# Sums of squares in one bf16 record each, and a scheduler that reckons with longer transfers

## The chip, the cores and the metric

The kernel runs on one core of a Trainium2 chip. The metric is the device time of one execution in microseconds; the median of three runs counts.

## What is computed

Attention with capped scores, then a gated feed-forward block with a token shift, then a block that mixes tokens by a rotated copy of the input. Batch 4, 12 heads, sequence 448, head size 64, model width 768, inner width 1024.

```python
scores = cap * tanh(q @ k.T / sqrt(64) / cap)
x = softmax(scores) @ v                       # heads side by side: (4, 448, 768)
xk = mu_k * x + (1 - mu_k) * x_prev           # x_prev: x one token earlier
xr = mu_r * x + (1 - mu_r) * x_prev
x = sigmoid(xr @ w_r) * (relu(xk @ w_k) ** 2 @ w_v)
theta = x @ w_theta
u = x + w_tok_r @ (x * cos(theta)) + w_tok_i @ (x * sin(theta))
out = u + relu(u @ w_ch)
```

## The kernel before, in words

The weights arrive as 64-bit words that hold floating-point numbers of double width. `group` loads a block of 768 KB (512 KB for w_v), rebases the high halves (`bits`, L455 on ScalarE, L457 on POOL, L459 on VectorE), and forms f32 values with three VectorE operations (L462, L465, L468). It then needs the size of the block: the sum of its squares. Where `early` is set (w_k, and v of the first batch) `grams` forms products of the values with themselves on TensorE in bf16 (L483), VectorE takes the diagonal's sum (L487), and a matmul with a matrix of ones adds over the partitions and gives every partition the total (L489). Elsewhere `squares` has ScalarE square the values with an accumulating column for each part (L496), and one f32 matmul for each column, accumulated, does the same (L501): one part for w_r, w_th and w_ch, two for w_v and for v of the later batches, seven for the token matrices. `size` (L508 to L512) takes a power of two from the exponent of that total; only the magnitude matters. With it the block is split into two f16 parts (L301, L296 or L305 for the first, L545 for the second).

All sums use one PSUM tile (`c_ps`), which the softmax sums (L678, L682, L714) share. Every product with a weight is three f16 matmuls of 448 columns: L785 to L787 for w_k, w_r and w_v, L959 to L961 for w_theta, L989 to L991 for the token matrices, L1011 to L1013 for w_ch. The scores and the products with v are f32 matmuls (L651, L655, L700, L703, L726, L729).

Two word buffers (`w_s`) serve all loads of words in turn. The results of the first phase (squared k, gate z, product x) go to memory and come back later (kd, zd, xd).

The order of everything comes from a planner that runs when the kernel is built. Each operation is registered with `op`: its engine, or a choice of engines, its duration, a rank, and the buffers it reads and writes. `Plan.order` plays the operations through in time, taking for each engine that is free the ready operation of lowest rank; DMA operations go one after the other through a pipe (`moved`), and their consumers are ready `LAT["DMA"]` after the transfer is through. The resulting sequence is issued as it stands: each engine, and SP's queue, which issues nearly all transfers, works through its part in that order. The durations in `op` thus set no time on the chip, but they set the order.

The lines that decide about transfers and about the sums:

```python
LAT = {"PE": 0.2, "ACT": 0.16, "DVE": 0.15, "POOL": 0.16, "DMA": 1.6, "SYS": 0.0}
issue = self.ISSUE.get(got.name, 0.48)
moved = max(t + issue, moved) + got.dur
heapq.heappush(events, (moved + self.LAT[e], seq, 1, got))
```

Of the kernel before, what the change touches and what calls it, by code (L numbers as in the profile page):

```python
# [10 lines left out]
BF16 = mybir.dt.bfloat16  # L11
U32 = mybir.dt.uint32
AF = mybir.ActivationFunctionType
ALU = mybir.AluOpType
# [67 lines left out]
class Plan:  # L82
# [3 lines left out]

    LAT = {"PE": 0.2, "ACT": 0.16, "DVE": 0.15, "POOL": 0.16, "DMA": 1.6, "SYS": 0.0}
    COLS = {"av": 1.0}
# [194 lines left out]
def body(nc, tc, exact, first, qk, v, cap, mu_k, mu_r, w_k, w_v, w_r, w_th, w_tr, w_ti, w_ch, out):  # L283
# [55 lines left out]
    unit = cpool.tile([128, 1], F32, name="unit")  # L339
    nc.gpsimd.memset(unit, 1.0)  # L340
    ones = cpool.tile([128, 3, 2, 32], F32, name="ones")
    nc.gpsimd.memset(ones, 0.0)
# [106 lines left out]
    def bits(rank, h, l, f, into, n, word, fb, res, after=()):  # L449
# [22 lines left out]
        return op("DVE", v1(n), rank, b3, r=[fb, word], w=[res], name="wb3")  # L472

    def grams(rank, parts, d):


        ps = Buf(c_ps)
        for i, sub in enumerate(parts):
            def gram(i=i, sub=sub):
                for k, (_, val, n, w) in enumerate(sub):  # L480
                    x = val().bitcast(BF16).rearrange("p (n two) -> p n two", two=2)[:, :, 1]
                    for c in range(0, n, w):
                        nc.tensor.matmul(ps.t[0:w, 0:w], x[:, c:c + w], x[:, c:c + w], start=(i == 0 and k == 0 and c == 0),  # L483
                                         stop=(i == len(parts) - 1 and k == len(sub) - 1 and c == n - w))
            op("PE", sum(0.06 * (n // w) for _, _, n, w in sub) + 0.1, rank, gram, r=[b for b, *_ in sub], w=[ps], name="gram")
        w = parts[0][0][3]
        op("DVE", v1(128), rank, lambda: nc.vector.scalar_tensor_tensor(out=junk[0:w, 0:w], in0=ps.t[0:w, 0:w], scalar=1.0, in1=ident[0:w, 0:w], op0=ALU.mult, op1=ALU.mult,  # L487
                                                                             accum_out=d.t[0:w]), r=[ps], w=[d], name="tiny")
        op("PE", 0.3, rank, lambda: nc.tensor.matmul(ps.t[:, 0:1], unit[0:w].to_broadcast([w, 128]), d.t[0:w], start=True, stop=True), r=[d], w=[ps], name="bcast")  # L489
        return ps  # L490

    def squares(rank, parts, d, after=()):

        ps = Buf(c_ps)
        for a, (f, val, n, dead, place) in enumerate(parts):
            op("ACT", act(n) + 0.19, rank, lambda a=a, val=val, place=place: nc.scalar.activation(out=place(), in_=val(), func=AF.Square, accum_out=d.t[:, a:a + 1]),  # L496
               r=[f] if f not in dead else [], w=[*dead, (d, a)], after=after, name="norm")

        def total():
            for a in range(len(parts)):  # L500
                nc.tensor.matmul(ps.t[:, 0:1], unit.to_broadcast([128, 128]), d.t[:, a:a + 1], start=(a == 0), stop=(a == len(parts) - 1))  # L501
        op("PE", 0.2 + 0.1 * len(parts), rank, total, r=[d], w=[ps], name="bcast")
        return ps
# [12 lines left out]
    def group(rank, src, dst, m, inv, nb, after=(), early=False):  # L516
# [3 lines left out]
        for a in range(len(dst)):  # L520
            w, f = Buf(w_s), Buf(f_s)
            vals.append(f)

            def half(i, w=w):
                return w.t[:, 0:2 * n].bitcast(U32).rearrange("p (n two) -> p n two", two=2)[:, :, i]

            def val(f=f):
                return f.t[:, 0:n]

            def ld(w=w, a=a):  # L530
                nc.sync.dma_start(out=w.t[:, 0:2 * n].bitcast(U32).rearrange("p (i n) -> p i n", i=nb),
                                  in_=src[n * a:n * a + n, 256 * m:256 * m + 256].rearrange("(i p) n -> p i n", p=128))
            op("DMA", 0.03 + n / 350, rank - 12, ld, w=[w], after=[o_open1], name="wld")
            bits(rank, lambda h=half: h(1), lambda h=half: h(0), val, val, n, w, f, f)
            parts.append((f, val, n, 128) if early else (f, lambda val=val: val().rearrange("p (i t n) -> p i t n", i=nb, t=2), n, [(dst[a], (m, 0)), (dst[a], (m, 1))],
                                                                     lambda a=a: dst[a].t[:, :, :, 128 * m:128 * m + 128].bitcast(F32)))
# [25 lines left out]
    for b in range(B):  # L562
# [4 lines left out]
        for c in range(2):  # L567
            t = Buf(w_s)
            op("DMA", 0.03 + n / 700, R - 10, lambda t=t, c=c, vb=vb: nc.sync.dma_start(out=t.t, in_=vb[:, c * n:(c + 1) * n]), w=[t], after=[o_open1], name="ldm")
            parts.append([(t, lambda t=t: t.t, n, 128)] if b == 0 else (t, lambda t=t: t.t, n, [t], lambda t=t: t.t))  # L570
# [21 lines left out]
    def inputs(g):  # L592
# [4 lines left out]
        else:  # L597
            op("DMA", 1.3, A - 30, lambda: nc.sync.dma_start(out=t.t, in_=qk[g].rearrange("p (t s) -> p t s", t=2)), w=[t], after=[o_open1], name="ldqk")
        vn = vnb[g] = Buf(vn_s)
        op("DMA", 0.8, A - 14, lambda: nc.sync.dma_start(out=vn.t[0], in_=v[g].rearrange("p (h c d) -> p h c d", h=2, c=KC)), w=[(vn, 0)], after=[o_open1], name="ldv")  # L600

# [6 lines left out]
    def largest_scores(g):  # L608
# [21 lines left out]
        def halves():  # L630
            for i in range(2):
                nc.sync.dma_start(out=mb.t[1][64 * i:64 * i + 64], in_=md[g].t[:, SH * i:SH * i + SH].rearrange("h (o s) -> o h s", o=1).to_broadcast([64, 2, SH]))
        op("DMA", 0.65, A + 5, halves, r=[md[g]], w=[(mb, 1)], name="rbi")

# [156 lines left out]
    for b in range(B):  # L791
        def taps(i):
            return [((hi, lo), lambda hi=hi: hi.t, lambda lo=lo: lo.t) for hi, lo in (mixed[i, b, j] for j in range(KD))]
        for m, ps in units("kmm", b, wk, KF, taps(0), PAIR * NP * (b + 1), gone, PAIR * NP / 14):
# [10 lines left out]
            op({"ACT": act(S) + 0.09, "DVE": v1(S)}, 0, 0.0, sq, w=[a, (acc[b], m)], name="sq")  # L805
            kend.append(op("DMA", 0.65, 0.0, lambda a=a, t=kd[b][m]: nc.sync.dma_start(out=t.t, in_=a.t), r=[a], w=[kd[b][m]], name="dst"))
        for m, ps in units("rmm", b, wr, KD, taps(1), PAIR * NP * (b + 1 + KF / 14), gone, PAIR * NP / 14):
            o_ = Buf(tmp_s)
            op({"ACT": act(S), "DVE": 0.62}, 0, 0.0, lambda e, ps=ps, o_=o_: copy(e, o_.t, ps.t[:, 0:S]), r=[ps], w=[o_], name="zev")
            op("DMA", 0.65, 0.0, lambda o_=o_, t=zd[b][m]: nc.sync.dma_start(out=t.t, in_=o_.t), r=[o_], w=[zd[b][m]], name="dst")  # L810
        atop = small()
# [53 lines left out]
    def tokens(rank):  # L865
        fo = []
        for i in range(KT):
            raw, f = Buf(w_s), Buf(xf_s)
            parts = {3: ((w_tr, 384, 64, 0), (w_ti, 0, 64, 64))}.get(i, ((w_tr, 128 * i, 128, 0) if i < 3 else (w_ti, 128 * i - 448, 128, 0),))
            for src, r0, rows, p0 in parts:  # L870
                op("DMA", 0.03 + rows * S * 8 / 360e3, rank - 12, lambda src=src, r0=r0, rows=rows, p0=p0, raw=raw: nc.sync.dma_start(
                    out=raw.t[p0:p0 + rows, 0:2 * S].bitcast(U32), in_=src[r0:r0 + rows]), w=[(raw, p0)], after=[o_open1], name="wld")
# [22 lines left out]
    def values(b):  # L895
        scaled(0.0, iv, ia[b], vsc[b])
        k2 = []
        for m in range(KF):
            a, k = Buf(ka_s), Buf(k2_s)
            k2.append(((k,), lambda k=k: k.t[:, 0], lambda k=k: k.t[:, 1]))  # L900
            rk = K20 + 100 * b + m
            op("DMA", 0.65, rk - 100, lambda a=a, t=kd[b][m]: nc.sync.dma_start(out=a.t, in_=t.t), r=[kd[b][m]], w=[a], after=[o_r2], name="lda")
            op(cs(S), 0, rk, lambda e, a=a, k=k, b=b: copy(e, k.t[:, 0], a.t, sa[b].t), r=[a, sa[b]], w=[(k, 0)], after=[o_r2], name="k2h")
            op("DVE", v1(S) + 0.06, rk, lambda a=a, k=k, b=b: nc.vector.scalar_tensor_tensor(
                out=k.t[:, 1], in0=a.t, scalar=sa[b].t, in1=k.t[:, 0], op0=ALU.mult, op1=ALU.subtract), r=[a, (k, 0), sa[b]], w=[(k, 1)], name="k2l")
        for m, ps in units("vmm", b, wv, KD, k2, VM0 + VM1 * b, []):
            z = Buf(z_s)
            op("DMA", 0.65, T2 - 110, lambda z=z, t=zd[b][m]: nc.sync.dma_start(out=z.t, in_=t.t), r=[zd[b][m]], w=[z], after=[o_l2], name="ldz")
            op("ACT", act(S) + 0.1, 1605.2 + 100 * b, lambda z=z, b=b, m=m: nc.scalar.activation(out=z.t, in_=z.t, func=AF.Sigmoid, scale=rho[b].t[:, m:m + 1]),
# [3 lines left out]
               r=[ps, vsc[b]], w=[z], name="x")  # L913
            op("DMA", 0.65, 0.0, lambda z=z, t=xd[b][m]: nc.sync.dma_start(out=t.t, in_=z.t), r=[z], w=[xd[b][m]], name="stx")
            op("DVE", v1(S), 0.0, lambda z=z, b=b, m=m: nc.vector.tensor_reduce(out=xmx[b].t[:, m:m + 1], in_=z.t, axis=AX.X, op=ALU.max, apply_absolute_value=True),
# [23 lines left out]
    def gates(b, ms, rk):  # L939
        for m in ms:  # L940
            x, h = Buf(xg_s), Buf(xs_s)
            xs[b, m] = h
            op("DMA", 0.65, rk - 10, lambda x=x, m=m: nc.sync.dma_start(out=x.t, in_=xd[b][m].t), r=[xd[b][m]], w=[x], after=[o_r2], name="ldx")
            op(cs(S), 0, rk, lambda e, x=x, h=h: copy(e, h.t[:, 0], x.t, sxi[b].t), r=[x, sxi[b]], w=[(h, 0)], after=[o_l2], name="xh")
# [3 lines left out]
    def angles(b, m):  # L948
        rk = T2 + ST * (6 * b + m)
        ps, x = Buf(q_ps), Buf(xf_s)  # L950
        xf[b, m] = x
        op("DMA", 0.65, rk - 25, lambda: nc.sync.dma_start(out=x.t, in_=xd[b][m].t), r=[xd[b][m]], w=[x], after=[o_r2], name="ldx")
        for kk in range(KD):
# [48 lines left out]
    def channels(b, ms):  # L1002
        for m in ms:
# [12 lines left out]
            op(tt(S), 0, rk, lambda e, t=t, x=x: e.tensor_tensor(out=x.t, in0=t.t, in1=x.t, op=ALU.add), r=[t], w=[x], name="res")  # L1016
            fin.append(op("DMA", 0.65, rk, lambda x=x, m=m: nc.sync.dma_start(out=out[m, :, b * S:(b + 1) * S], in_=x.t), r=[x], name="sto"))

# [76 lines left out]
```

## Time and profile before

| | |
|---|---|
| median of three runs | 803.93 us (803.72 to 804.85) |
| profiled execution | 807.98 us, span 806.2 us |
| mean granted TensorE clock | 0.991 |
| TensorE matmul busy | 777.0 us, 96% of the span, 4924 records |
| TensorE weight load busy | 388.7 us, 48% |
| VectorE, ScalarE, POOL busy | 563.5 us (70%), 430.2 us (53%), 105.0 us (13%) |
| DMA engines busy | 46.9% of 16 engines, 114.76 MB moved |
| v loads (256 KB), xd stores, ka loads (224 KB) | 2.7, 2.3, 3.8 us from issue to landing |
| ScalarE's waits for w_ch loads | 19.0 us in five |

Matmuls are pipelined, so the records' busy times overlap and a busy TensorE need not be at its peak. One f32 matmul leaves two records, one f16 or bf16 matmul one. A granted clock of 1.00 is 2.4 GHz; the lower level is 1.2 GHz.

### The profile page before, as it was taken

The page shows a single profiled execution, that of the slowest core. Times are in us where ns is not written, and L with a number is a line of the kernel's source. Part 1 is how long each engine was busy: PE and PEld are TensorE (multiplying, and loading weights), DVE is VectorE, ACT ScalarE, POOL GpSimd, SP SyncE. Part 2 cuts the span into 40 slices and gives each one's busy share as a digit, 9 for nine tenths or more (in the row PEclk, how much of TensorE's full clock was granted, in tenths as well). Part 3 has the DMA queues.
Part 4 walks back from the last instruction along what each step waited for, and adds up shares of the span by engine and source line. Part 5 has one row for each costly group of instructions (what it writes and reads, how often), then busy time and mean ns, then how long its engine had stood idle before and what let it go on. Part 6 is the DMA issues. An engine that isn't in the chain of part 4 may idle for free.

```text
span 806.2 us, 12778 instructions
## 1 busy us (share of the span) xinstructions
PE 777.0 (96%) x4924; PEld 388.7 (48%) x4924; DVE 563.5 (70%) x1023; ACT 430.2 (53%) x653; POOL 105.0 (13%) x114
## 2 busy tenths in 40 slices
PE   5999999999999999999999998999999999999997
PEld 2445455454444444444545544555555555555553
DVE  2878778888787899778866868777655545545531
ACT  4979868678575785655435443454635333232201
POOL 1224312320012031103000110100301000000000
PEclk9999999999999999999999999999999999999999
DMA  7754646336343333403667866553525433334412
GB/s 262 232 192 128 208 146 226 127 115 196 125 149 126 100 123 126 163 35 111 202 196 257 270 212 226 162 160 82 126 51 133 92 92 86 82 75 100 95 34 72
DMA packets 116829, 114.76 MB, mean 142 GB/s; under 512 B 55820, under 2 KB 108824, under 8 KB 116760
## 3 DMA queue, kind: packets, MB, share of 16 engines
q1 hardware_dynamic: 116592, 113.86, 46.9%
q8 instruction: 40, 0.66, 0.4%
q14 instruction: 29, 0.24, 0.1%
q10 hardware_dynamic: 168, 0.01, 0.0%
HBM read 78.98 MB, written 23.86 MB: 128 GB/s over the span
## 4 chain that ended last, share of the span: by engine, by line
PE 82%; DVE 7%; DMA 7%; ACT 2%; issue 1%; SPq 0%; POOL 0%; DVEq 0%; ACTq 0%; POOLq 0%
PE one L785 10%; PE one L787 9%; PE one L786 9%; PE big L655 6%; PE q L991 4%; PE q L990 4%; PE q L989 4%; PE one L726 4%; PE one L1013 3%; PE one L1012 3%; PE one L1011 3%; PE one L700 3%; PE q L960 2%; PE q L961 2%; PE q L959 2%; DMA w<-in_w_ch 2%
## 5 line engine op out<-in xcount | busy, mean ns | idle before, releaser
L664 ACT ACTIVATE th<-big,tsc 128x896 f32<-128x896 f32 x72 | 70.2, 1004 | 30.1 <-PE big L655 29.8
L668 ACT ACTIVATE th<-th,cap_t 128x896 f32<-128x896 f32 x72 | 73.3, 1038 | 0.0
L785 PE MATMUL one<-k,wv 128*128 128x448 f16 x192 | 68.3, 356 | 1.7 <-DVE z L911 1.4
L785 PE MATMUL one<-sl,wk 128*128 128x448 f16 x192 | 68.1, 355 | 1.6 <-ACT g L796 1.2
L787 PE MATMUL one<-sl,wk 128*128 128x448 f16 x192 | 68.1, 355 | 0.5 <-DVE wk L545 0.5
L787 PE MATMUL one<-k,wv 128*128 128x448 f16 x192 | 68.3, 356 | 0.0
L786 PE MATMUL one<-k,wv 128*128 128x448 f16 x192 | 68.3, 356 | 0.0
L786 PE MATMUL one<-sl,wk 128*128 128x448 f16 x192 | 68.0, 354 | 0.2 <-POOL sl L760 0.2
L989 PE MATMUL q<-wo,zt 128*128 128x448 f16 x168 | 59.2, 352 | 0.0
L991 PE MATMUL q<-wo,zt 128*128 128x448 f16 x168 | 59.2, 352 | 0.0
L990 PE MATMUL q<-wo,zt 128*128 128x448 f16 x168 | 59.2, 352 | 0.0
L1015 ACT ACTIVATE z<-one,scal 128x448 f32<-128x448 f32 x24 | 15.1, 628 | 71.8 <-PE one L1013 71.8
L785 PE MATMUL one<-sl,wr 128*128 128x448 f16 x144 | 51.0, 354 | 0.7 <-ACT wr L496 0.4
L787 PE MATMUL one<-sl,wr 128*128 128x448 f16 x144 | 50.7, 352 | 0.7 <-ACT wr L496 0.7
L786 PE MATMUL one<-sl,wr 128*128 128x448 f16 x144 | 50.7, 352 | 0.0
L655 PE MATMUL big<-qk 64*64 64x448 f32 x432 | 50.0, 564 | 0.0
L975 DVE SCALAR_TENSOR_TENSOR cs<-xf,scal,cs 128x896 f32<-128x896 f32 x24 | 27.6, 1149 | 28.9 <-DMA xf<-xd 23.9
L455 ACT ACTIVATE w<-w 128x768 f32<-128x768 f32 (+2 forms) x26 | 21.9, 840 | 41.1 <-DMA w<-in_w_ch 19.0
L720 DVE RECIPROCAL xt<-one 128x448 f32<-128x448 f32 x12 | 35.5, 2958 | 11.7 <-PE one L714 11.7
L1016 DVE TENSOR_TENSOR xf<-z,xf 128x448 f32<-128x448 f32 x24 | 15.0, 624 | 34.7 <-ACT z L1015 34.7
L993 DVE SCALAR_TENSOR_TENSOR xf<-q,scal,xf 128x448 f32<-128x448 f32 x24 | 16.4, 683 | 32.3 <-PE q L991 32.1
L1012 PE MATMUL one<-w_u,wc 128*128 128x448 f16 x108 | 38.1, 352 | 0.0
(204 smaller groups left out, 1752.0 us busy)
## 6 DMA issues: line engine op xcount, KB each, us to landing
qk<-in_qk SPq DMA_DIRECT2D x18, 448.0 KB, 3.8
kd<-g SPq DMA_DIRECT2D x32, 224.0 KB, 3.7
vn<-in_v SPq DMA_DIRECT2D x24, 256.0 KB, 2.7
w<-in_v SPq DMA_DIRECT2D x8, 768.0 KB, 4.3
w<-in_w_k SPq DMA_DIRECT2D x8, 768.0 KB, 5.2
w<-in_w_v SPq DMA_DIRECT2D x12, 512.0 KB, 4.4
zd<-tmp SPq DMA_DIRECT2D x24, 224.0 KB, 1.9
z<-zd SPq DMA_DIRECT2D x24, 224.0 KB, 2.8
```

What stands on the lines that cost most here:

```text
L655: nc.tensor.matmul(ps.t[o, h, 0:S], t.t[p, 1, 128 * c + 64 * i:128 * c + 64 * i + 64], t.t[p, 0], start=True, stop=True)
L664: op("ACT", act(n * S) + 0.08, A + 1 + 1.8 * c, lambda src=src, th=th: nc.scalar.activation(out=th.t, in_=src(), func=AF.Tanh, scale=tsc), ...
L668: op("ACT", act(n * S) + 0.08, A + 3 + 1.8 * c, lambda th=th: nc.scalar.activation(out=th.t, in_=th.t, func=AF.Exp, scale=cap_t), w=[th], ...
L720: nc.vector.reciprocal(out=rs(), in_=rs() if exact else sp.t[:, 0:S])
L726: nc.tensor.matmul(ps.t[64 * h:64 * h + 64, 0:S], vn.t[0][:, h, c], th[c].t[:, h], start=(c == 0), stop=False, skip_group_check=True)
L785: nc.tensor.matmul(ps.t[:, 0:S], wh, xh(), start=(kk == 0), stop=False)
L786: nc.tensor.matmul(ps.t[:, 0:S], wh, xl(), start=False, stop=False)
L787: nc.tensor.matmul(ps.t[:, 0:S], wl, xh(), start=False, stop=(kk == len(xs) - 1))
L989: nc.tensor.matmul(o, z.t[:, 0, i], wo[i].t[:, 0], start=(i == 0), stop=False)
L990: nc.tensor.matmul(o, z.t[:, 1, i], wo[i].t[:, 0], start=False, stop=False)
L991: nc.tensor.matmul(o, z.t[:, 0, i], wo[i].t[:, 1], start=False, stop=(i == KT - 1))
L1012: nc.tensor.matmul(ps.t[:, 0:S], wh, u.t[:, 1], start=False, stop=False)
```

## The change

The matmul that adds over partitions, at L489 and in `squares`, takes bf16 operands in place of f32: a bf16 matrix of ones, and the upper half of the f32 column, read as bf16 (`upper`). Where `squares` has several columns, VectorE first adds them into one, in place of one accumulating matmul for each. The durations that the planner is told for these matmuls go to 0.11. Separately, the planner's `LAT["DMA"]` goes from 1.6 to 2.0, and the durations of most transfers go up by 12 to 21%; those of the transposes, of the small ones and of the v halves stay.

```diff
-    LAT = {"PE": 0.2, "ACT": 0.16, "DVE": 0.15, "POOL": 0.16, "DMA": 1.6, "SYS": 0.0}
+    LAT = {"PE": 0.2, "ACT": 0.16, "DVE": 0.15, "POOL": 0.16, "DMA": 2.0, "SYS": 0.0}
...
+    unitb = cpool.tile([128, 1], BF16, name="unitb")
+    nc.gpsimd.memset(unitb, 1.0)
...
+    def upper(d):
+        return d.t[:, 0:1].bitcast(BF16)[:, 1:2]
...
-        op("PE", 0.3, rank, lambda: nc.tensor.matmul(ps.t[:, 0:1], unit[0:w].to_broadcast([w, 128]), d.t[0:w], start=True, stop=True), r=[d], w=[ps], name="bcast")
+        op("PE", 0.11, rank, lambda: nc.tensor.matmul(ps.t[:, 0:1], unitb[0:w].to_broadcast([w, 128]), upper(d)[0:w], start=True, stop=True), r=[d], w=[ps], name="bcast")
...
-        def total():
-            for a in range(len(parts)):
-                nc.tensor.matmul(ps.t[:, 0:1], unit.to_broadcast([128, 128]), d.t[:, a:a + 1], start=(a == 0), stop=(a == len(parts) - 1))
-        op("PE", 0.2 + 0.1 * len(parts), rank, total, r=[d], w=[ps], name="bcast")
+        if len(parts) > 1:
+            tiny(rank, lambda: nc.vector.tensor_reduce(out=d.t[:, 0:1], in_=d.t[:, 0:len(parts)], axis=AX.X, op=ALU.add), w=[d])
+        op("PE", 0.11, rank, lambda: nc.tensor.matmul(ps.t[:, 0:1], unitb.to_broadcast([128, 128]), upper(d), start=True, stop=True), r=[d], w=[ps], name="bcast")
...
-            op("DMA", 0.03 + n / 350, rank - 12, ld, w=[w], after=[o_open1], name="wld")
+            op("DMA", 0.03 + n / 290, rank - 12, ld, w=[w], after=[o_open1], name="wld")
```

The other durations of transfers, which the planner alone reads:

| transfer | before | after |
|---|---|---|
| whole v for its size (ldm) | 0.03 + n/700 | 0.03 + n/580 |
| qk (ldqk) | 1.3 | 1.5 |
| v of a group (ldv) | 0.8 | 0.9 |
| token matrices (wld) | rows * S * 8 / 360e3 | rows * S * 8 / 300e3 |
| every 224 KB transfer (dst, lda, ldz, stx, ldx, sto) | 0.65 | 0.78 |

## Rows read from the trace of the kernel before

**Rows 1.** The page's chain that ended last: shares of the span by engine.
```profile
PE 82%; DVE 7%; DMA 7%; ACT 2%; issue 1%; SPq 0%; POOL 0%; DVEq 0%; ACTq 0%; POOLq 0%
```
**Rows 2.** Busy us of each engine by stretch, instructions, granted clock, DMA share, GB/s.
```profile
17.00:161.00 144.00, 136.40 (x1229) 70.72 (x1228) 119.04 (x233) 114.70 (x157) 41.60 (x38) 0.96 0.56 182
161.00:370.00 209.00, 208.62 (x1401) 93.44 (x1402) 173.74 (x265) 139.37 (x212) 28.84 (x26) 1.00 0.38 123
370.00:490.00 120.00, 112.95 (x596) 59.20 (x594) 89.83 (x196) 57.09 (x106) 14.25 (x16) 0.99 0.71 226
490.00:800.00 310.00, 310.00 (x1643) 161.15 (x1642) 176.55 (x313) 111.41 (x172) 18.01 (x13) 1.00 0.40 99
...
480.00:500.00 20.00, 16.92 (x81) 8.33 (x80) 16.67 (x46) 7.38 (x12) 2.77 (x3) 0.91 0.69 233
```
**Rows 3.** TensorE's waits: line, what released it, us in total, times, longest.
```profile
PE one L483 <- DMA w<-in_v: 4.4, 1, 4.4
...
PE q L960 <- DVE xs L945: 3.0, 1, 3.0
PE one L678 <- DVE scal L508: 1.8, 3, 1.3
PE one L501 <- ACT wr L496: 1.6, 1, 1.6
...
PE one L489 <- DVE junk L487: 1.2, 3, 0.4
```
**Rows 4.** The chain that ended last, in order of time, 370 to 495 us.
```profile
469.32 8.20 DMA w<-in_w_ch
```
**Rows 5.** ScalarE's timeline, 455 to 486 us: start, duration, instruction, [idle before].
```profile
477.55 0.91 ACT L455 ACTIVATE w<-w 128x768 f32<-128x768 f32 x1 [4.68 <-DMA w<-in_w_ch]
```
**Rows 6.** Groups of instructions by line: the sums' records.
```profile
L501 PE MATMUL one<-scal,unit 128*128 128x1 f32 x86 | 11.9, 232 | 2.2 <-ACT wr L496 1.6 <-DVE scal L508 0.3 <-ACT wc L496 0.3
...
L489 PE MATMUL one<-scal,unit 128*128 128x1 f32 x18 | 3.2, 249 | 1.2 <-DVE junk L487 1.2
```
**Rows 7.** TensorE's timeline: a gram, and four sums with what follows each.
```profile
28.24 0.52 PE L483 MATMUL one<-f 128*128 128x128 bf16 x6
...
96.59 0.38 PE L489 MATMUL one<-scal,unit 128*128 128x1 f32 x2
96.90 0.98 PE L655 MATMUL big<-first 64*64 64x448 f32 x8
...
117.97 0.28 PE L489 MATMUL one<-scal,unit 128*128 128x1 f32 x2
118.11 0.35 PE L785 MATMUL one<-sl,wk 128*128 128x448 f16 x1
...
135.89 0.50 PE L501 MATMUL one<-scal,unit 128*128 128x1 f32 x4
136.25 0.35 PE L785 MATMUL one<-sl,wr 128*128 128x448 f16 x1
...
430.40 1.62 PE L501 MATMUL one<-scal,unit 128*128 128x1 f32 x14
432.09 0.35 PE L785 MATMUL one<-k,wv 128*128 128x448 f16 x1
```
**Rows 8.** Groups of instructions by line: VectorE's reciprocal and smallest reduction.
```profile
L720 DVE RECIPROCAL xt<-one 128x448 f32<-128x448 f32 x12 | 35.5, 2958 | 11.7 <-PE one L714 11.7
...
L423 DVE TENSOR_REDUCE scal<-scal 128x1 f32<-128x8 f32 (+2 forms) x9 | 1.4, 157 | 0.4 <-ACT g L802 0.3
```
**Rows 9.** DMA issues: KB each, median us from issue to landing.
```profile
qk<-in_qk SPq DMA_DIRECT2D x18, 448.0 KB, 3.8
...
w<-in_w_k SPq DMA_DIRECT2D x8, 768.0 KB, 5.2
...
w<-in_w_th SPq DMA_DIRECT2D x6, 768.0 KB, 4.4
w<-in_w_ch SPq DMA_DIRECT2D x6, 768.0 KB, 7.6
```

More of the change, by code (lines that the diff above doesn't have):

```diff
@@ L568, in body @@
             t = Buf(w_s)
-            op("DMA", 0.03 + n / 700, R - 10, lambda t=t, c=c, vb=vb: nc.sync.dma_start(out=t.t, in_=vb[:, c * n:(c + 1) * n]), w=[t], after=[o_open1], name="ldm")
+            op("DMA", 0.03 + n / 580, R - 10, lambda t=t, c=c, vb=vb: nc.sync.dma_start(out=t.t, in_=vb[:, c * n:(c + 1) * n]), w=[t], after=[o_open1], name="ldm")
             parts.append([(t, lambda t=t: t.t, n, 128)] if b == 0 else (t, lambda t=t: t.t, n, [t], lambda t=t: t.t))
@@ L597, in inputs @@
         else:
-            op("DMA", 1.3, A - 30, lambda: nc.sync.dma_start(out=t.t, in_=qk[g].rearrange("p (t s) -> p t s", t=2)), w=[t], after=[o_open1], name="ldqk")
+            op("DMA", 1.5, A - 30, lambda: nc.sync.dma_start(out=t.t, in_=qk[g].rearrange("p (t s) -> p t s", t=2)), w=[t], after=[o_open1], name="ldqk")
         vn = vnb[g] = Buf(vn_s)
-        op("DMA", 0.8, A - 14, lambda: nc.sync.dma_start(out=vn.t[0], in_=v[g].rearrange("p (h c d) -> p h c d", h=2, c=KC)), w=[(vn, 0)], after=[o_open1], name="ldv")
+        op("DMA", 0.9, A - 14, lambda: nc.sync.dma_start(out=vn.t[0], in_=v[g].rearrange("p (h c d) -> p h c d", h=2, c=KC)), w=[(vn, 0)], after=[o_open1], name="ldv")
         def halves():
@@ L632, in halves @@
                 nc.sync.dma_start(out=mb.t[1][64 * i:64 * i + 64], in_=md[g].t[:, SH * i:SH * i + SH].rearrange("h (o s) -> o h s", o=1).to_broadcast([64, 2, SH]))
-        op("DMA", 0.65, A + 5, halves, r=[md[g]], w=[(mb, 1)], name="rbi")
+        op("DMA", 0.78, A + 5, halves, r=[md[g]], w=[(mb, 1)], name="rbi")
     def scores(g):
@@ L805, in body @@
             op({"ACT": act(S) + 0.09, "DVE": v1(S)}, 0, 0.0, sq, w=[a, (acc[b], m)], name="sq")
-            kend.append(op("DMA", 0.65, 0.0, lambda a=a, t=kd[b][m]: nc.sync.dma_start(out=t.t, in_=a.t), r=[a], w=[kd[b][m]], name="dst"))
+            kend.append(op("DMA", 0.78, 0.0, lambda a=a, t=kd[b][m]: nc.sync.dma_start(out=t.t, in_=a.t), r=[a], w=[kd[b][m]], name="dst"))
         for m, ps in units("rmm", b, wr, KD, taps(1), PAIR * NP * (b + 1 + KF / 14), gone, PAIR * NP / 14):
@@ L809, in body @@
             op({"ACT": act(S), "DVE": 0.62}, 0, 0.0, lambda e, ps=ps, o_=o_: copy(e, o_.t, ps.t[:, 0:S]), r=[ps], w=[o_], name="zev")
-            op("DMA", 0.65, 0.0, lambda o_=o_, t=zd[b][m]: nc.sync.dma_start(out=t.t, in_=o_.t), r=[o_], w=[zd[b][m]], name="dst")
+            op("DMA", 0.78, 0.0, lambda o_=o_, t=zd[b][m]: nc.sync.dma_start(out=t.t, in_=o_.t), r=[o_], w=[zd[b][m]], name="dst")
         atop = small()
@@ L870, in tokens @@
             for src, r0, rows, p0 in parts:
-                op("DMA", 0.03 + rows * S * 8 / 360e3, rank - 12, lambda src=src, r0=r0, rows=rows, p0=p0, raw=raw: nc.sync.dma_start(
+                op("DMA", 0.03 + rows * S * 8 / 300e3, rank - 12, lambda src=src, r0=r0, rows=rows, p0=p0, raw=raw: nc.sync.dma_start(
                     out=raw.t[p0:p0 + rows, 0:2 * S].bitcast(U32), in_=src[r0:r0 + rows]), w=[(raw, p0)], after=[o_open1], name="wld")
@@ L901, in values @@
             rk = K20 + 100 * b + m
-            op("DMA", 0.65, rk - 100, lambda a=a, t=kd[b][m]: nc.sync.dma_start(out=a.t, in_=t.t), r=[kd[b][m]], w=[a], after=[o_r2], name="lda")
+            op("DMA", 0.78, rk - 100, lambda a=a, t=kd[b][m]: nc.sync.dma_start(out=a.t, in_=t.t), r=[kd[b][m]], w=[a], after=[o_r2], name="lda")
             op(cs(S), 0, rk, lambda e, a=a, k=k, b=b: copy(e, k.t[:, 0], a.t, sa[b].t), r=[a, sa[b]], w=[(k, 0)], after=[o_r2], name="k2h")
@@ L907, in values @@
             z = Buf(z_s)
-            op("DMA", 0.65, T2 - 110, lambda z=z, t=zd[b][m]: nc.sync.dma_start(out=z.t, in_=t.t), r=[zd[b][m]], w=[z], after=[o_l2], name="ldz")
+            op("DMA", 0.78, T2 - 110, lambda z=z, t=zd[b][m]: nc.sync.dma_start(out=z.t, in_=t.t), r=[zd[b][m]], w=[z], after=[o_l2], name="ldz")
             op("ACT", act(S) + 0.1, 1605.2 + 100 * b, lambda z=z, b=b, m=m: nc.scalar.activation(out=z.t, in_=z.t, func=AF.Sigmoid, scale=rho[b].t[:, m:m + 1]),
@@ L913, in values @@
                r=[ps, vsc[b]], w=[z], name="x")
-            op("DMA", 0.65, 0.0, lambda z=z, t=xd[b][m]: nc.sync.dma_start(out=t.t, in_=z.t), r=[z], w=[xd[b][m]], name="stx")
+            op("DMA", 0.78, 0.0, lambda z=z, t=xd[b][m]: nc.sync.dma_start(out=t.t, in_=z.t), r=[z], w=[xd[b][m]], name="stx")
             op("DVE", v1(S), 0.0, lambda z=z, b=b, m=m: nc.vector.tensor_reduce(out=xmx[b].t[:, m:m + 1], in_=z.t, axis=AX.X, op=ALU.max, apply_absolute_value=True),
@@ L942, in gates @@
             xs[b, m] = h
-            op("DMA", 0.65, rk - 10, lambda x=x, m=m: nc.sync.dma_start(out=x.t, in_=xd[b][m].t), r=[xd[b][m]], w=[x], after=[o_r2], name="ldx")
+            op("DMA", 0.78, rk - 10, lambda x=x, m=m: nc.sync.dma_start(out=x.t, in_=xd[b][m].t), r=[xd[b][m]], w=[x], after=[o_r2], name="ldx")
             op(cs(S), 0, rk, lambda e, x=x, h=h: copy(e, h.t[:, 0], x.t, sxi[b].t), r=[x, sxi[b]], w=[(h, 0)], after=[o_l2], name="xh")
@@ L951, in angles @@
         xf[b, m] = x
-        op("DMA", 0.65, rk - 25, lambda: nc.sync.dma_start(out=x.t, in_=xd[b][m].t), r=[xd[b][m]], w=[x], after=[o_r2], name="ldx")
+        op("DMA", 0.78, rk - 25, lambda: nc.sync.dma_start(out=x.t, in_=xd[b][m].t), r=[xd[b][m]], w=[x], after=[o_r2], name="ldx")
         for kk in range(KD):
@@ L1016, in channels @@
             op(tt(S), 0, rk, lambda e, t=t, x=x: e.tensor_tensor(out=x.t, in0=t.t, in1=x.t, op=ALU.add), r=[t], w=[x], name="res")
-            fin.append(op("DMA", 0.65, rk, lambda x=x, m=m: nc.sync.dma_start(out=out[m, :, b * S:(b + 1) * S], in_=x.t), r=[x], name="sto"))
+            fin.append(op("DMA", 0.78, rk, lambda x=x, m=m: nc.sync.dma_start(out=out[m, :, b * S:(b + 1) * S], in_=x.t), r=[x], name="sto"))
     for b in range(B):
```

## Prediction, written before the changed kernel was run

> **What bounds the kernel now.** The chain of waits comes first: TensorE carries 82% of it, transfers 7% and VectorE 7% [rows 1]. So a microsecond counts when it is TensorE's, and only where TensorE isn't waiting for something else. The busy time by stretch says where that is [rows 2]. From 161 to 370 us and from 490 to 800 us TensorE has next to no idle time (209.00 - 208.62 = 0.4 us, and nothing). From 17 to 161 us it idles 144.00 - 136.40 = 7.6 us, beside a VectorE busy for 83% and a ScalarE for 80%; from 370 to 490 us it idles 7.05 us, beside DMA engines busy for 71%. The list of TensorE's waits names the releasers [rows 3]: 4.4 us at the start, which the change doesn't touch, then 3.0 us for xs near 486 us, 1.8 us for the size arithmetic (L508), 1.6 us for a norm of w_r (L496), and a tail of small ones.
>
> **The two large waits.** Both follow a load of words. In the first, ScalarE's rebase of w_r (L455) waits for its load, the square (L496) comes behind it, and TensorE's sum starts 1.6 us late [rows 3]. In the second, a w_ch load is issued at 469.32 us and lands some 8.20 us later [rows 4]; ScalarE, an in-order queue, waits 4.68 us for it until 477.55 [rows 5], with the k copies queued behind, VectorE's halves of k behind those, and then the xs that TensorE needs, 3.0 us late [rows 3]. The slice from 480 to 500 us has a granted clock of 0.91 [rows 2]: part of it ran at the 1.2 GHz level after that idle time, which gives away 20 x 0.09 = 1.8 us more. Together 1.6 + 3.0 + 1.8 = 6.4 us.
>
> **Part 1: the sums' records.** 52 f32 matmuls of one column (18 records at L489, 86 at L501, two to a matmul [rows 6]) become 37 bf16 ones of one record: 9 behind grams, 28 behind squares. The records' own 11.9 + 3.2 us overlap, so I take distances from a sum's start to the next start [rows 7]: a two-record sum costs 0.14 us between f16 matmuls (117.97 to 118.11) and 0.31 us beside f32 ones (96.59 to 96.90); there are 27 of them, by the neighbours about 6.5 us. Nine four-record sums cost 0.36 to 0.53 us (135.89 to 136.25 is typical), 3.6 us. The fourteen-record one costs 1.69 us (430.40 to 432.09). Sum: 11.8 us, of it 4.6 from 17 to 161 us (17 sums), 2.8 from 161 to 370 (7), 4.1 from 370 to 490 (11), 0.3 later (2).
>
> No one-column bf16 sum is in the trace. The nearest row is a gram: six bf16 records of 128 columns take 0.52 us, 0.087 each [rows 7]. Half of the f32 prices is 0.07 and 0.155. I take 0.10 us: 37 x 0.10 = 3.7 us, so 8.1 us less TensorE time (2.9, 2.1, 3.0 and 0.1 by stage). At 0.07 it is 9.2 us; with one record as dear as today's two (37 x 0.25 us) it is 2.6 us.
>
> What of this reaches the end? From 161 to 370 us and after 490 us TensorE never rests: all 2.2 us. In the other two stages it rests 5 to 6% of the time, each time for an engine or a load that a shorter sum doesn't hasten; a sum ahead of such a wait only lengthens the wait. I count half, 5.9 / 2 = 2.95 us; the ends are 0 and 5.9. Part 1 brings **-5.15 us**.
>
> **Part 2: the added reduction.** Ten of the 28 sums behind squares have several columns and get a VectorE reduction first. The nearest one takes 157 ns (L423) [rows 8]: 1.6 us in all, which costs nothing by itself where VectorE has slack (83% busy from 161 to 370 us, where seven of the ten stand). But the sum now waits for VectorE's queue instead of ScalarE alone. Queued ahead there can be an L720 reciprocal of 2958 ns [rows 8], and behind the waiting sum stand all of TensorE's matmuls. The nearest row is the gram's sum, which also waits for a VectorE operation (L487): 1.2 us of TensorE idle over nine sums [rows 3]. So 10 x 0.13 = **+1.3 us**; the ends are 0 and ten waits like the longest of TensorE's for the size arithmetic, 1.3 us each, 13 us [rows 3].
>
> The shared PSUM tile of the sums is freed earlier by the same shortening; the softmax sums that waited 1.8 us for L508 want that tile [rows 3]. I cost it at nothing, since VectorE, whose turn they wait for, gains nothing. At most 1.8 us could go.
>
> **Part 3: the scheduler's transfers.** No instruction is added; the order on every queue is worked out anew: TensorE's, VectorE's, ScalarE's and SP's, and with the choice of engine POOL's too. A 768 KB load is reckoned at 0.48 + 0.03 + 768/290 + 2.0 = 5.16 us instead of 4.30; measured medians are 5.2 (w_k), 4.4 (w_th) and 7.6 us (w_ch). A qk load goes from 3.38 to 3.98 us, measured 3.8 [rows 9]; a v load from 2.88 to 3.38, measured 2.7 (the table of the profile). So the new figures are nearer for the loads of words and of qk, and too long for v. That is what the two large waits ask for: with a later landing reckoned, work that is ready is put ahead of the rebase in ScalarE's queue. But w_ch still lands 2.4 us later than reckoned. I count half of the 6.4 us, **-3.2 us**. The bounds: all of it goes (-6.4), or a new order opens a hole as dear as both in another place (+6.4).
>
> The Trainium skill, "DMA: Bandwidth & Descriptors", section "Latency and other measured facts", gives an HBM access latency of 0.2 us on average and 2 us at high load, and calls it the dominant component of a transfer's fixed cost. The trace agrees in kind: the same 768 KB take 4.4 us as w_th and 7.6 us as w_ch [rows 9]. By that rule one longer constant doesn't follow the crowded stretch, and part 3 would bring nothing; that case is the first rival.
>
> **Sum.** -5.15 + 1.3 - 3.2 = -7.05 us. Durations are from an execution of 807.98 us (span 806.2 us and 1.8 us around it), 4.05 us above the median of 803.93; that execution would come to 800.9, and taken from the median the forecast is 796.9, say **797.0 us**. The terms miss by about 3 us each way in part 1 (none or all of the contested 5.9 us), 3.2 in part 3 (none or all of the 6.4) and 1.5 in part 2; as independent misses that is 4.6 us, so its own range is 792.5 to 801.5.
>
> **Rivals.** First, the loads still land later than reckoned where the DMA engines are crowded; both large waits stay, and only the sums pay: 803.93 - 5.15 + 1.3 = 800.1. For it: 7.6 us for w_ch against 5.16 reckoned. Against: w_r's load, on which the other wait hangs, is like w_k's 5.2 us.
>
> Second, slower: words pass through two buffers, so a load can start only when the conversion two before it has read its words. If conversions are ordered later by the added 0.86 us, each also starts the next load but one later. The 14 loads of w_k and w_r fall before 161 us, where TensorE already waits for what they yield [rows 3]: 14 x 0.86 / 2 = 6.0 us, part 3's gain is gone, and 803.93 - 3.85 + 6.0 = 806.1. It decides the sign once a load is set back by more than 3.85 / 7 = 0.55 us. For it: a w_k load takes 5.2 us [rows 9], and the buffers leave only one other load to overlap it. Against: ScalarE and VectorE have 17 to 20% of slack there [rows 2].
>
> Third, no difference: the savings from 17 to 161 and 370 to 490 us fall into waits wholly and the reductions cost what I took: -2.2 + 1.3 = -0.9, 803.0.
>
> Fourth, everything pays: -8.1 + 1.3 - 6.4 = -13.2, 790.7.
>
> **Chances.** Forecast 0.46, loads still late 0.18, slower conversions 0.17, no difference 0.10, everything 0.09. Of the second rival's neighbourhood some orders are worse than 806.1, so I let the range run from 790.5 to 807. A measurement of this kernel tells 0.2%, 1.6 us, from no change. Faster: 0.46 + 0.09 and 0.15 of the first rival's 0.18, 0.70; within it the third rival and the rest of the first, 0.13; slower 0.17.
>
> **What would show it.** Right, part 1: 37 bf16 records of one column and no f32 one at these lines, under 0.16 us from start to next start, and some 8 us less TensorE busy time. Part 2: TensorE waits on VectorE ahead of the sums of 1 to 2 us in total. Part 3: no TensorE wait of 3 us ahead of the xs matmuls, granted clock 1.00 near 490 us, and ScalarE's waits for w_ch under today's 19.0 us (the table of the profile). Wrong, if TensorE's idle time from 17 to 161 us grows past 7.6 us (slower conversions), if a new wait of several microseconds stands where the w_v or token words are wanted, or if sums stand idle behind reciprocals.

## The result, and the profile after

The changed kernel takes 794.21 us (791.74 to 794.83, four runs) against 804.39 us for the kernel before (803.72 to 805.09): a ratio of 0.9865, 95% interval 0.984 to 0.9891. On a second chip it is 0.9876 (0.9827 to 0.9925, 795.44 against 803.99 us). The forecast was 797.0 us, 7 us less; 8.6 to 10.2 us were measured.

The profiled execution took 794.37 us, its span is 792.5 us. The chain that ended last has moved further to TensorE, at the cost of transfers and VectorE [rows 1]:

```profile
PE 86%; DVE 5%; DMA 4%; ACT 2%; issue 1%; SPq 0%; POOL 0%; ACTq 0%; DVEq 0%
```

Busy time by stretch, with the columns of [rows 2] (the last two are granted clock and DMA, as there):

```profile
17.00:161.00 144.00, 134.10 (x1267) 67.21 (x1260) 118.65 (x230) 120.79 (x167) 44.70 (x39) 1.00 0.57 183
161.00:370.00 209.00, 206.20 (x1344) 88.83 (x1344) 170.00 (x262) 138.07 (x215) 36.72 (x38) 1.00 0.39 127
370.00:490.00 120.00, 117.36 (x614) 60.25 (x613) 95.04 (x221) 60.84 (x111) 9.24 (x11) 0.99 0.73 234
490.00:786.00 296.00, 296.00 (x1569) 153.48 (x1568) 165.19 (x274) 107.21 (x168) 21.45 (x13) 1.00 0.39 97
480.00:500.00 20.00, 20.00 (x111) 10.55 (x109) 16.56 (x47) 7.21 (x13) 1.56 (x2) 1.00 0.53 166
```

TensorE's idle time from 370 to 490 us fell from 7.05 to 2.6 us, and the slice from 480 to 500 us is full, at a clock of 1.00. Against that, idle time from 17 to 161 us grew from 7.6 to 9.9 us, and from 161 to 370 us from 0.4 to 2.8. The list of waits shows which went and which came [rows 3]; here L699 is the spread of the softmax denominators (L694 before), L965 the xs product, L507 the sum behind squares:

```profile
PE one L699 <- DVE rs L694: 5.4, 4, 1.9
PE big L660 <- DMA first<-in_qk: 4.0, 1, 4.0
PE one L489 <- DMA w<-in_v: 2.8, 2, 1.5
PE big L660 <- ACT th L669: 1.4, 1, 1.4
...
PE q L965 <- DVE xs L950: 1.0, 2, 0.5
...
PE one L507 <- DVE scal L513: 0.7, 1, 0.7
```

Both large waits that the prediction named are gone as such (3.0 us for xs is 1.0, the sum's 1.6 us for w_r's square is no longer there). A new one, 5.4 us for the reciprocal of the denominators, has taken the place of waits that came to 0.6 us before.

The sums themselves, by line and then in TensorE's timeline, each with what follows it [rows 6, 7]:

```profile
L507 PE MATMUL one<-scal,unitb 128*128 128x1 bf16 x28 | 4.7, 169 | 0.7 <-DVE scal L513 0.7
...
L506 DVE TENSOR_REDUCE scal<-scal 128x1 f32<-128x2 f32 (+1 forms) x10 | 1.4, 144 | 2.4 <-ACT wo L502 1.7 <-ACT w L502 0.7
...
L495 PE MATMUL one<-scal,unitb 128*128 128x1 bf16 x9 | 1.6, 175 | 0.0
```

```profile
95.42 0.18 PE L495 MATMUL one<-scal,unitb 128*128 128x1 bf16 x1
95.53 0.98 PE L660 MATMUL big<-first 64*64 64x448 f32 x8
...
119.84 0.17 PE L507 MATMUL one<-scal,unitb 128*128 128x1 bf16 x1
119.87 0.35 PE L790 MATMUL one<-sl,wk 128*128 128x448 f16 x1
...
230.40 0.17 PE L507 MATMUL one<-scal,unitb 128*128 128x1 bf16 x1
230.50 0.97 PE L731 MATMUL one<-th,vn 128*64 128x448 f32 x4
```

37 records where there were 104. Between f16 matmuls a sum now costs 0.03 us, beside f32 ones 0.10 to 0.11.

**A sum over the whole span.** Three parts make up a span: TensorE's work at full clock (its busy time less what the lower clock added to it), that clock loss, and idle time. The loss is counted only where TensorE was busy; in both traces the granted clock is low again after the last matmul, and that costs nothing. Kernels with the same sums give 767.9 to 770.2 us of work (52 two-record matmuls, three kernels) and 759.9 to 762.0 (37 one-record ones, eight executions of six kernels): a figure from one execution holds to some 2 us, and a difference of two to some 3.

| | span | busy | clock | work at full clock | clock loss + idle |
|---|---|---|---|---|---|
| before | 806.2 | 777.0 | 0.991 | 770.2 | 6.8 + 29.2 = 36.0 |
| changed | 792.5 | 763.5 | 0.994 | 760.1 | 3.4 + 29.0 = 32.4 |

By these two executions 10.1 us less work and 3.6 us less waiting; by the means of those three and eight, 769.4 and 760.7, it is 8.7 us less work. The steps from each sum's records to the next start, waits left out, come to 10.9 us before and 2.0 in the changed kernel, 8.9 us less. Either way it looks like a gain made by the sums alone. The experiments show that it isn't.

### The profile page after: what moved, and what is told of

It is laid out like the page before. It is cut to its first block, busy times and chain, and to the rows that moved or that the text cites. A ratio compares the mean times of both kernels' runs of the same rounds, so it can differ in the third digit from the quotient of the medians.

```text
span 792.5 us, 12657 instructions
## 1 busy us (share of the span) xinstructions
PE 763.5 (96%) x4857; PEld 374.4 (47%) x4857; DVE 555.2 (70%) x1010; ACT 435.9 (55%) x669; POOL 114.5 (14%) x122
## 4 chain that ended last, share of the span: by engine, by line
PE 86%; DVE 5%; DMA 4%; ACT 2%; issue 1%; SPq 0%; POOL 0%; ACTq 0%; DVEq 0%
PE one L790 12%; PE one L792 11%; PE one L791 11%; PE big L660 6%; PE q L995 4%; PE q L996 4%; PE q L994 4%; PE one L1018 3%; PE one L1017 3%; PE one L1016 3%; PE one L731 3%; PE one L705 2%; PE q L964 2%; PE q L965 2%; PE q L966 2%; DMA w<-in_v 2%
## 5 line engine op out<-in xcount | busy, mean ns | idle before, releaser
L984 POOL TENSOR_TENSOR zb<-cs,zb 128x896 f16<-128x896 f32 x9 | 17.3, 1923 | 169.4 <-DVE zb L303 88.2
L765 POOL TENSOR_TENSOR sl<-mx,sl 128x448 f16<-128x448 f32 x27 | 31.9, 1183 | 67.5 <-ACT sl L299 64.8
```

Of the source, the lines that this page charges most:

```text
L765: op(tt(S, True), 0, R + i, lambda e, t=t, hi=hi, lo=lo: e.tensor_tensor(out=lo.t, in0=t.t, in1=hi.t, op=ALU.subtract), r=[t, hi], w=[lo], ...
```

## The experiments

Two theories stood against each other at first: the sums' work pays (records), or the order worked out with longer transfers pays (order). A third came with them: that any new order lies a few microseconds off the last, and the changed kernel is one draw (luck). All ratios are to the kernel before, run on the same chip.

**Sums alone.** The diff without the lines on transfers.

> The kernel before with the one-record sums alone, planner told their new durations, transfers reckoned as before. Records theory (the sums' TensorE time is what pays, the order is a side effect of either sign): 795 to 799 us. Order theory (the longer transfers make the better order and carry most of the gain): 800 to 804 us. Luck theory (any new order moves the time by several us either way): no value, 794 to 806.

Measured: 800.48 us, 0.9965 (0.9948 to 0.9982). That is inside the range of the order theory, 1.5 us above that of the records theory, and by the ratios 7 to 8 us short of the changed kernel.

**Transfers alone.** The kernel before with

```diff
-    LAT = {... "DMA": 1.6, ...}
+    LAT = {... "DMA": 2.0, ...}
-            op("DMA", 0.03 + n / 350, rank - 12, ld, w=[w], after=[o_open1], name="wld")
+            op("DMA", 0.03 + n / 290, rank - 12, ld, w=[w], after=[o_open1], name="wld")
```

and the other lengths of the table.

> The kernel before with the longer transfers in the planner alone, f32 sums. Records theory: 802 to 806 us, no change that counts. Order theory: 796 to 800 us, and no wait of 3 us for xs near 486 us. My term for this part was -3.2 us: 800.7 us by it.

Measured: 806.21 us, 1.0032 (1.0007 to 1.0058), a little slower. That is outside the range of the order theory. ScalarE's waits for words (L455) did fall, as the change intends: 13.8 us in all, where the kernel before has 39.0. The time didn't follow. In this trace 5.7 us of TensorE idle time stand from 360 to 380 us, where the kernel before has 0.7.

So apart the halves come to 0.9965 x 1.0032 = 0.9997, together to 0.9865.

**One-record sums in the old order.** The planner is told nothing new, so every instruction keeps its place.

```diff
-                nc.tensor.matmul(ps.t[:, 0:1], unit.to_broadcast([128, 128]), d.t[:, a:a + 1], ...)
+                nc.tensor.matmul(ps.t[:, 0:1], unitb.to_broadcast([128, 128]), upper(d, a), ...)
```

> Every instruction in the order of the kernel before; each of the 52 f32 one-column matmuls becomes a bf16 one of one record (two for two parts, seven for seven, so no VectorE reduction is added). By the changed kernel's trace such a sum costs 0.03 us between f16 matmuls and 0.11 beside f32 ones, which leaves about 2.5 of 11.8 us. Records theory with all of it reaching the end: 795 us. With my half of it in the stretches where TensorE waits: 798 to 799 us. Luck theory: 799 or more, since the order is unchanged.

Measured: 800.61 us, 0.9974 (0.9952 to 0.9996). Work at full clock is 762.5 us in this execution, 7.7 us less than in that of before; the time fell by 2.1 us (0.3 to 3.9). By these figures about three quarters of the saved work must have turned into waiting. That is inferred: the two traced executions themselves lie 10.6 us apart, since before's, 807.98 us, is slower than the four runs of the result above (803.72 to 805.09) and this one, 797.39 us, is the second fastest of ten. What they show is that TensorE's idle time from 360 to 500 us is 8.8 us here, where it was 7.05, and that the xs wait of [rows 3] still stands there:

```profile
PE q L965 <- DVE xs L950: 2.8, 1, 2.8
```

**Two-record sums in the new order.** The changed kernel, order and reductions as they are, with f32 operands:

```diff
-    ... nc.tensor.matmul(ps.t[:, 0:1], unitb.to_broadcast([128, 128]), upper(d), start=True, stop=True) ...
+    ... nc.tensor.matmul(ps.t[:, 0:1], unit.to_broadcast([128, 128]), d.t[:, 0:1], start=True, stop=True) ...
```

> Every instruction in the order of the changed kernel, the added VectorE reductions too, but the 37 sums are f32 matmuls of two records. They cost 0.14 to 0.31 us instead of 0.03 to 0.11, 37 x 0.15 = 5.5 us more TensorE time. Records theory: 797 to 800 us. Order theory: 795 to 796 us, hardly above the changed kernel.

Measured: 796.05 us, 0.9916 (0.9891 to 0.9941), between the two ranges. The work is 766.8 us, 6.7 more than with bf16 by these two executions (5.4 by the steps from the sums' records to the next start), yet against the changed kernel's 0.9865 and 0.9876 only 0.4 to 0.5% are lost, 3 to 4 us, with intervals that touch or overlap. The new order with f32 sums and fewer records (37 x 2 for 52 x 2) brings 6.8 us. Those steps come to 7.4 us here and 10.9 in the kernel before, so up to 3.5 of the 6.8 us can be the fewer records' and not the order's.

**Neighbours of the changed kernel.** On one chip: the changed kernel again (0.9876, above), then with only the landing of 2.0, only the longer lengths, and with

```diff
-        op("PE", 0.11, rank, lambda: nc.tensor.matmul(ps.t[:, 0:1], unitb...
+        op("PE", 0.13, rank, lambda: nc.tensor.matmul(ps.t[:, 0:1], unitb...
```

> The changed kernel as it is, beside its neighbours on one chip. All theories: 10 us under the kernel before, ratio 0.984 to 0.989.

> One-record sums, and of the planner's longer transfers only the landing (1.6 to 2.0); the lengths stay as before. Transfers theory (a reckoning nearer to the measured landings shortens the waits for words, whichever half of it): 795 to 798 us, between the sums alone (0.9965 of the kernel before) and the changed kernel. Luck theory (any re-sorted order lies somewhere within some 8 us): no value, 794 to 804.

> One-record sums, and of the planner's longer transfers only the lengths (a sixth more); the landing stays at 1.6. Transfers theory: 795 to 799 us and ScalarE's and VectorE's waits for words between those of the sums alone (31.5 + 11.3 us) and of the changed kernel (19 + 3 us). Luck theory: no value, 794 to 804.

> The changed kernel with the planner told 0.13 instead of 0.11 for each one-record sum, which means nothing on the chip but sorts the work anew in each queue. Transfers theory: within 2 us of the changed kernel, since sums and transfers are as there. Luck theory: 3 to 8 us above it, since the changed kernel is one good draw among many.

Measured: landing alone 799.13 us, 0.992 (0.989 to 0.995); lengths alone 790.21 us, 0.9809 (0.9758 to 0.9859), the fastest of all; 0.13 instead of 0.11 800.86 us, 0.9962 (0.9941 to 0.9984). The transfers theory missed all three: the landing alone came out 1 us above its range, with 42.7 us of ScalarE's waits for words where the sums alone have 31.5, and the lengths alone 5 us below it, below the luck theory's range too. The last one shows what an order without meaning can do: a figure that only the planner reads, changed by 0.02, takes the ratio on that chip from 0.9876 to 0.9962, 5.4 us by the medians and 6.9 by the ratios, most of the changed kernel's gain. Sums and transfers are reckoned as before it; even the waits for words are as low (19.6 us on ScalarE, 18.8 in the changed kernel). What differs is a hole. Busy time from 360 to 400 us with the columns of [rows 2], first the changed kernel, then this one:

```profile
360.00:400.00 40.00, 37.77 (x195) 18.74 (x192) 33.06 (x67) 22.61 (x47) 5.66 (x6) 0.96 0.52 167
...
360.00:400.00 40.00, 30.95 (x158) 15.29 (x156) 32.20 (x67) 24.33 (x51) 6.16 (x6) 0.91 0.46 150
```

TensorE idles 2.2 us there in the one and 9.05 in the other; from 17 to 161 us it is 9.9 and 11.2. TensorE's waits in the kernel with 0.13 from 355 to 420 us:

```profile
PE one L790 <- ACT sl L299: 7.6, 1, 7.6
PE one L791 <- DVE sl L765: 0.5, 1, 0.5
PE one L790 <- DVE tmp L303: 0.4, 1, 0.4
PE one L791 <- POOL sl L765: 0.4, 1, 0.4
```

It stands where attention ends and the second weight product begins: the last token-shift mixes, which the w_k products want, queue on ScalarE and VectorE behind the split of k for the product after it (L301, L909).

**The hole closed by hand.** In that kernel, after planning, the k splits go behind the last mixes in both queues. The edit also moves those loads of k (`lda`) that stood behind the first of these splits, so the expectation's "nothing else moves" doesn't hold for SP's queue.

```diff
+    mix = [o for o in P.ops if o.name in ("mxd", "mxk", "mxh", "mxl")][-7:]
+    lo, hi = seq.index(last1[-1]), max(seq.index(o) for o in mix)
+    k2 = [i for i in range(lo, hi) if seq[i].name in ("k2h", "k2l")]
+    late = [seq[i] for i in range(lo, hi) if i in k2 or (seq[i].name == "lda" and i > k2[0])] if k2 else []
+    seq = seq[:lo] + [o for o in seq[lo:hi + 1] if o not in late] + late + seq[hi + 1:]
```

> The kernel whose planner was told 0.13 for the sums (800.9 us, a hole of 7.6 us in TensorE near 366 us), with one edit of the order after planning: the two f16 parts of k of the next phase that stood ahead of the last token-shift mixes in ScalarE's and VectorE's queues go behind them; nothing else moves. If the order near the border of the phases is what makes that draw bad, the hole falls to 3 to 4 us and the time to 796 to 798 us. If the hole is only where some other lateness shows, it moves and the time stays within 1.6 us of 800.9.

Measured: 804.65 us, 1.0018 (0.9996 to 1.0039), worse instead of better: 3.8 us by the medians, 4.5 by the ratios (the two ran on different chips). TensorE's waits in the same stretch:

```profile
PE one L790 <- ACT g L801: 6.6, 1, 6.6
PE one L790 <- ACT sl L299: 3.7, 1, 3.7
PE one L790 <- DVE tmp L303: 0.4, 1, 0.4
PE one L791 <- POOL sl L765: 0.4, 1, 0.4
```

The hole shrank to 3.7 us as expected, and a larger one opened behind it, where the products' evictions (L801, ScalarE) now stand behind the k splits. My expectation was wrong in its sum: moving work out of the way in one place of an in-order queue put it in the way in the next. ScalarE's queue wasn't full there, though: it idled 3.3 us, as two pairs of splits ahead of that eviction waited for their loads:

```profile
375.55 1.25 ACT L301 ACTIVATE k<-first,scal 128x448 f16<-128x448 f32 x2 [2.31 <-DMA first<-kd]
377.75 1.23 ACT L301 ACTIVATE k<-ka,scal 128x448 f16<-128x448 f32 x2 [0.95 <-DMA ka<-kd]
378.88 0.62 ACT L801 ACTIVATE g<-one,scal 128x448 f32<-128x448 f32 x1
```

The four k loads behind the first four are issued from 373.01 us on, where they were issued from 365.94 on before the edit: k has four buffers, so a load must wait for the splits (L301 and L909) that read its buffer, and it now went back with them. The two holes also cost clock. From 360 to 400 us TensorE idles 11.3 us, and part of the rest runs at the 1.2 GHz level, with f16 matmuls 0.37 us apart instead of 0.19; the granted clock is 0.79 where it was 0.91:

```profile
360.00:400.00 40.00, 28.72 (x132) 13.36 (x131) 29.56 (x56) 21.48 (x44) 5.66 (x5) 0.79 0.41 132
```

Over the whole span idle time even fell, from 34.6 to 33.4 us, and the clock loss of busy time rose from 1.7 to 5.9: by these two executions what the edit cost is the clock's. The runs point the same way: their granted clocks are 0.983 to 0.990, where those before the edit are 0.987 to 0.994.

**The same for the kernel before, and records in the fastest order.** The kernel before with 0.32 and 0.22 + 0.1 for each part in place of 0.3 and 0.2 + 0.1; the lengths-only kernel with f32 sums in its own order; and that kernel again beside them.

> The kernel before, its planner told 0.02 more for each of these sums, which means nothing on the chip. Luck theory: off the kernel before by 2 to 7 us either way, more likely slower, since that one was kept among others. Against it: within 1.6 us.

> The order of the kernel with longer lengths alone (landing 1.6), instruction by instruction, but with f32 sums of two records. Records theory: the 37 second records and their price cost 6.5 us of TensorE time by the accounting of the earlier traces (765.2 against 758.7 us at full clock); in that order TensorE waits least, so most of it reaches the end: 4 to 6 us above its twin with one-record sums. If the order alone made that kernel fast, it is within 2 us of its twin.

> The kernel with one-record sums and longer lengths alone, again, beside its f32 twin. All theories: 0.976 to 0.986 of the kernel before, the fastest of those tried.

Measured: the kernel before re-sorted 808.21 us, 1.005 (1.0026 to 1.0074). Lengths alone 790.01 us, 0.9813 (0.9781 to 0.9844); the same order with f32 sums 790.07 us, 0.9813 (0.9781 to 0.9845). Here the second records cost nothing that can be measured. Busy time of the two from 17 to 161 and from 360 to 500 us, first with f32 sums:

```profile
17.00:161.00 144.00, 137.34 (x1293) 71.76 (x1293) 123.48 (x233) 121.05 (x173) 41.32 (x36) 1.00 0.60 187
...
360.00:500.00 140.00, 134.83 (x717) 71.09 (x715) 110.00 (x251) 66.26 (x119) 19.93 (x22) 0.99 0.68 217
```

then with one-record sums:

```profile
17.00:161.00 144.00, 136.18 (x1279) 68.65 (x1279) 122.58 (x231) 120.73 (x172) 41.07 (x36) 0.99 0.60 187
...
360.00:500.00 140.00, 134.85 (x709) 69.04 (x708) 110.75 (x254) 67.08 (x119) 19.42 (x22) 0.99 0.69 221
```

TensorE idles 6.7 us from 17 to 161 us with f32 sums and 7.8 us with bf16, and 5.2 us from 360 to 500 us with either. Over the whole span the traces give 765.1 us of work with f32, and 760.2 and 762.0 in the two executions of the kernel with bf16: 3.1 to 4.9 us of saved work (the 765.2 and 758.7 of the expectation take off the lower clock where TensorE idled too). The steps from the sums' records to the next start, 7.2 us with f32 and 1.8 with bf16, say 5.3. The spans are 789.8 us against 788.3 and 788.1, so in these executions 1.5 to 1.7 us of it came through, and clock loss and idle time took the rest. The medians, which don't rest on that division, say that all of it came back as waiting, though their intervals leave room for some 3 us either way.

## Why the prediction came out right, point by point

**The direction and the range** held, and the forecast lies 1.6 to 2.8 us off. None of its three terms is borne out at its size: the first brought less in every fixed order, the second cost nothing that shows, and the third brought between what I took and twice that. These misses offset each other, so much of that closeness is chance.

**The sums' work** fell by more than I took: a one-record sum costs 0.03 us between f16 matmuls and 0.10 to 0.11 ahead of f32 ones, not 0.10 throughout, and the work at full clock fell by about 8.7 us (means over executions; 10.1 in the one pair) instead of 8.1. From start to start the 37 sums, their waits left out, come to 2.0 us. The 11.8 us that the prediction has for the sums before is 0.9 too much: by the same steps the 27 two-record sums come to 5.7 us and not 6.5, and 0.2 us of the fourteen-record sum's 1.69 is a wait of the next matmul; all 104 records come to 10.9. **What of it reaches the end** was over-sized at 5.15 us: in a fixed order it is 2.1 us of 7.7 (old order), 3 to 4 of 5.4 to 6.7 (new order, on different chips) and none of 3 to 5 (the fastest order), the times by ratios and medians and the work by single executions. The step that was off is the share: "all of it" where TensorE never rests, and half elsewhere. In the old order the runs can't tell which of the two failed; in the fastest order both did, within the intervals. My reading is that a stretch without idle time is only full because work is there to do; when it is done earlier, TensorE comes earlier to the next thing that it must wait for. The traces bear that out in part: in the old order idle time from 360 to 500 us grew by 1.8 us, in the fastest order that from 17 to 161 us by 1.2; the rest of the lost share has no place that was shown.

**The added reduction** shows no cost, where I took 1.3 us: ten of 144 ns, and no wait of TensorE in the list is for L506. The one wait of a sum, 0.7 us, is for L513.

**The order** was taken at -3.2 us: with f32 sums the new order brings 6.8 us, the reductions and fewer records included, so its own part lies between 3.3 and 6.8 us. The two waits that I named went as foretold, with ScalarE's waits for w_ch down from 19.0 to 12.9 us and a clock of 1.00 near 490 us. But the reason, transfers reckoned nearer to what they take, isn't what carries it: the same reckoning makes the kernel before 0.3% slower, and with the planner told 0.02 more for a sum it leaves 0.4% of the gain although the waits for words stay low.

**The rivals.** The one on late loads fell with the waits. The one on slower conversions was wrong in the time; the sign that the prediction gave for it did come, idle time from 17 to 161 us past 7.6 us, but it grew by 2.3 us and not 6, and through the reciprocal of the denominators (0.6 to 5.4 us), not through w_k. "No difference" (803.0 us) and "everything" (790.7 us) both lie outside what was measured. The sentence from the Trainium skill on latency under load ("DMA: Bandwidth & Descriptors", "Latency and other measured facts") fits what is left: w_ch still takes 7.0 us against w_th's 4.3 in the changed kernel, where the planner has one figure for both; no run here tells that latency from the time that other transfers take, and it decided nothing.

**What stays open.** Planned with one-record sums, five different orders came to 0.981 to 0.997 (the one altered by hand to 1.002); planned with f32 sums, the kernel before and two others to 1.000 to 1.005. The two groups don't overlap. That may be because the planner's figures for the sums are now nearer to the truth, or because there is less work, or chance; eight draws don't tell. And no single place was shown to make an order good: the one that was closed by hand opened another.

## What to carry to other kernels

Where a planner orders the work, price an edit twice: with the order held fixed, and re-planned beside a control in which a figure without meaning is changed by a hair. If the control moves the time by as much as the edit, as 0.13 for 0.11 did here with 5 to 7 us, the edit's gain can't be told from the draw's, and the thing to do is to draw more often: the best of these orders is 0.981 of the kernel before, 4 to 5 us under the changed kernel. And work taken from an engine that is busy for 96% of the time is not time won until its next wait has been looked up; between none and some 60% of it came through here.

## What the hardware showed beside that

A one-column bf16 matmul, with weights of its own to load, delays the f16 stream around it by only 0.03 us (119.84 to 119.87); the matmuls ahead of it keep their step of 0.19 us. The f32 sum's 0.14 us at such a place (117.97 to 118.11, [rows 7]) isn't two halves of 0.07 us, as the prediction has it. In the trace its second record starts 0.03 us after the first, just as the f16 matmul does after the bf16 sum, and the f16 matmul starts 0.11 us after the second. So what the change takes away at such a place is the second record's share. An f32 weight load takes 189 ns on average where the bf16 one takes 97; the first record's runs beside the f16 matmul ahead of it, and the second's has only that step of 0.03 us. That the load sets the 0.11 us is my reading; no run changes the load alone.

```profile
L507 PEld LDWEIGHTS <-unitb 128*128 128x128 bf16 x28 | 2.7, 97 | 4.7 <-issue 1.4 <-DVE scal L513 0.9 <-DVE mx L762 0.3
```

That line is of the changed kernel; its counterpart before, of L501, has 86 loads of 128x128 f32 and 13.2 us busy in all. Ahead of an f32 matmul the same bf16 instruction's step to the next start is 0.10 to 0.11 us, more than three times that ahead of an f16 one. It goes with what comes next: behind f32 matmuls and ahead of an f16 one the step is 0.03 to 0.04 us (283.88 to 283.91). What the f32 matmul would have lost there without the sum, no run shows.
